# Loading the first two batches' queries and keys in fp32 into unused accumulators, and writing out the order of the attention and first-expert steps

## The chip, the core and the metric

One core of a Trainium2 chip. The metric is the device time of one execution in microseconds (us); lower is better.

## The reference, cut to what matters

Attention with exponential features of both signs, then a mixture of eight experts whose weights P come from eight rounds of row and column normalisation.

```python
# q, k, v: (8 batches, 8 heads, 576, 64) fp32;  w_phi: (64, 128)
def phi(x):
    proj = einsum('bhsd,df->bhsf', x, w_phi)
    proj = proj - max(abs(proj), axis=-1)
    return concatenate([exp(proj), exp(-proj)], axis=-1)
q_p, k_p = phi(q), phi(k)
kv = einsum('bhsf,bhsd->bhfd', k_p, v);  z = sum(k_p, axis=2)
x = einsum(q_p, kv) / (q_p . z + 1e-6)          # reshaped to (4608, 512)
# P: softmax-like table (4608, 8), normalised 8 times over rows and columns
for e in range(8):
    out += P[:, e:e+1] * (maximum(x @ w1[e], 0) @ w2[e])   # 512 -> 1024 -> 512
```

## The kernel before

The kernel records every operation with an estimated duration and its dependencies in a plan. A list scheduler, run when the kernel is built, then writes the program: it repeatedly takes the operation that can start earliest by its model, and among equals the one recorded first. So each engine's instruction order is fixed at build time. It depends on the order of recording and on the modelled durations of everything, loads included. On the chip each engine runs its own list in order and waits where it must.

Work is cut into 32 pairs of heads (four per batch). The 576 rows are taken as 512 plus a rest of 64; the rests of a whole batch are handled together. For each pair: scores, maxima and exponentials of keys and queries (`pair_a`), GpSimd's products of v with the maxima's exponentials, the key-value sums and outputs (`pair_b`), and the transposed x (`pair_c`). Expert 0 runs between the pairs as fill: 24 "up" steps and 20 "down" steps.

```python
# loads: cast fp32 -> bf16 on the way, so issued from GpSimd, into 2 staging buffers
def load_qk(b, hh, nh, t, r=()):
    for x, src in ((1, k), (0, q)):
        dma("POOL", nh << 17, 230, lambda ...: nc.gpsimd.dma_start(
            out=t["qk"]()[:, x, o:o + nh], in_=src[b, hh:hh + nh, 0:SM]....))
ring(a_in, [128, 2, 4, NJ * D], BF16, "qk", 2)
...
# batches 0 and 1: transposed by TensorE in bf16; later batches by a DMA transpose
if b < 2:
    for x in (1, 0):
        ptr = new("P1")
        for c in range(4):
            pe(128, ... nc.tensor.transpose(bf(ptr)[:, c*128:(c+1)*128], t["qk"]()[...], ident) ...)
        dve(256, ... nc.vector.tensor_copy(out=t["T"]()[...], in_=bf(ptr)[:, 0:512]) ...)
...
# one fixed pattern of steps: a = pair_a (+ rest_a), e = one up and one down of expert 0
for i in range(NS + AD + 1):
    for s in "aebc":
        if s == "a" and i < NS: stage_a(i)
        elif s == "e" and i - LAG < 4 * NA + 4: expert0(i - LAG)     # LAG = 7
        elif s == "b": stage_b(i - AD)                                # AD = 1
        elif s == "c": stage_c(i - AD - 1)
```

The five accumulators `acc[0..4]` (128 x 4 x 512 fp32 each) lie unused until expert 0's first down step writes one.

## Time and profile before

| | before |
|---|---|
| time, median of 4 runs beside the changed kernel | 1053.74 us (1051.75 to 1054.75) |
| TensorE idle from 0 to 90 us | 21.5 us |
| GpSimd busy from 0 to 25 us | 21.7 us |
| second products of pair 0 / pair 8 / pair 31 start on GpSimd | 10.7 / 70.6 / 222.3 us |
| first matmul of expert 1's weights on x | 274.2 us |

All rows but the first come from one profiled execution of 1056.06 us.

The page of the kernel before, its span and first part (busy us and share of the span for TensorE = PE, its weight loads = PEld, VectorE = DVE, ScalarE = ACT, GpSimd = POOL):

```profile
span 1054.0 us, 24517 instructions
...
PE 1022.4 (97%) x9512; PEld 841.3 (80%) x9512; DVE 824.6 (78%) x1634; ACT 707.8 (67%) x1560; POOL 475.4 (45%) x551
...
```

The windows view of the kernel before. Columns are named in its first line; "PEclk" is the granted TensorE clock.

```profile
...
core 0: us, PE busy (x) PEld busy (x) DVE busy (x) ACT busy (x) POOL busy (x), PEclk, DMA share, GB/s
0.00:25.00 25.00, 14.51 (x136) 9.22 (x137) 14.80 (x35) 13.44 (x34) 21.69 (x42) 1.00 0.90 135
0.00:90.00 90.00, 68.45 (x734) 43.52 (x735) 72.69 (x179) 68.99 (x180) 66.48 (x128) 0.96 1.03 154
90.00:220.00 130.00, 128.71 (x1423) 83.68 (x1421) 116.37 (x284) 120.27 (x309) 79.38 (x159) 1.00 0.79 129
220.00:270.00 50.00, 48.55 (x308) 24.40 (x307) 42.29 (x114) 17.98 (x36) 3.25 (x6) 0.97 0.36 119
300.00:1054.00 754.00, 749.75 (x6834) 668.28 (x6831) 569.66 (x1021) 470.77 (x983) 320.45 (x254) 1.00 0.27 69
...
```

From 90 us on TensorE is nearly always busy. All that is loose lies in the first 90 us, where four engines are each at 74 to 81%. GpSimd is the one that is full at the very start: 21.7 of 25 us.

The chain of waits of the kernel before (start, length, what):

```profile
...
3.57 1.79 POOL qk_r L367 x3
5.36 6.26 DMA qk_r<-in_q_dram
...
19.66 0.61 POOL vrd_89 L440
...
46.76 0.97 POOL qk_r L367 x2
...
50.63 0.72 POOL qk_r L367
...
61.23 10.31 DMA qkT<-qk
...
```

TensorE's rests hang on a q load that GpSimd could only issue at 5.36 us, behind other loads, and that landed at 11.6 us. Then GpSimd's own products and load issues are on the chain at 20 us and at 46 to 51 us, and a DMA transpose at 61 to 71 us.

The clock's records in this trace show half clock until 15.4 us, again from 25.7 to 32.5 us and from 230.5 to 233.9 us. The view's PEclk column cannot show the first of these, since the records begin with the change to full clock; the pitch of the matmuls does (0.43 us per 512 columns, 0.22 later).

### The profile page before, as it was taken

What the parts mean: (1) busy time and instruction counts of PE and PEld (TensorE: products, weight loads), DVE (VectorE), ACT (ScalarE), POOL (GpSimd) and SP (SyncE); (2) the same over time, 40 slices, a digit from 0 to 9 for tenths busy, and PEclk for the clock granted to TensorE, in tenths of its full rate; (3) what the DMA queues carried; (4) which work ended last, traced back from release to release, by engine and by line L of the source; (5) the groups of instructions that cost most, each with busy time, mean ns of one, the idle gap of its engine ahead of it and who ended that gap; (6) DMA issues with size and microseconds to landing.
All of it is one profiled execution on the core that took longest, in us unless ns stands there. A gap on an engine that the chain in (4) does not pass through costs nothing.

```text
span 1054.0 us, 24517 instructions
## 1 busy us (share of the span) xinstructions
PE 1022.4 (97%) x9512; PEld 841.3 (80%) x9512; DVE 824.6 (78%) x1634; ACT 707.8 (67%) x1560; POOL 475.4 (45%) x551
## 2 busy tenths in 40 slices
PE   5889999999899999999999999999999999999998
PEld 3546666654588888888888888888888888888886
DVE  6889988988867787778877787778777877777775
ACT  5789989954896656666666666665666666666663
POOL 8776755510044344334444444444333544434442
PEclk9899999999999999999999999999999999999999
DMA  9998886914511133113411341116111521114333
GB/s 143 141 187 133 136 142 121 159 47 164 101 41 47 48 89 81 41 51 81 89 43 41 76 86 42 49 46 127 41 41 51 111 61 42 41 41 128 114 131 120
DMA packets 105236, 91.57 MB, mean 87 GB/s; under 512 B 45344, under 2 KB 80288, under 8 KB 105120
## 3 DMA queue, kind: packets, MB, share of 16 engines
q1 hardware_dynamic: 65040, 63.78, 22.3%
q0 software_dynamic: 40080, 26.23, 18.2%
q8 instruction: 74, 1.21, 0.5%
q14 instruction: 42, 0.34, 0.1%
HBM read 94.98 MB, written 14.16 MB: 104 GB/s over the span
## 4 chain that ended last, share of the span: by engine, by line
PE 89%; ACT 4%; DVE 3%; DMA 2%; POOL 1%; issue 1%; DVEq 0%; ACTq 0%; POOLq 0%
DVE m L376 1%; DMA qkT<-qk 1%; ACT U L1027 1%; DMA qk_r<-in_q_dram 1%; DVE xb L590 0%; PE P_13550 L999 0%; PE P_12438 L999 0%; PE P_8591 L999 0%; PE P_15513 L999 0%; PE P_14556 L999 0%; PE P_14095 L999 0%; PE P_13743 L999 0%; PE P_13392 L999 0%; PE P_13188 L999 0%; PE P_12788 L999 0%
## 5 line engine op out<-in xcount | busy, mean ns | idle before, releaser
L999 PEld LDWEIGHTS <-S 128*128 128x128 bf16 x1984 | 194.1, 98 | 22.9 <-issue 0.5
L999 PEld LDWEIGHTS <-T 128*128 128x128 bf16 x1512 | 147.9, 98 | 20.4 <-issue 3.2
L999 PEld LDWEIGHTS <-hT 128*128 128x128 bf16 x1488 | 145.6, 98 | 16.9
L907 DVE TENSOR_TENSOR S<-hT 128x1024 bf16<-128x1024 bf16 x124 | 80.3, 684 | 0.0
L1155 POOL TENSOR_TENSOR acc_77<-acc_77,V 128x512 f32<-128x512 f32 x28 | 36.3, 1308 | 54.6 <-ACT V L1152 54.5
L1155 POOL TENSOR_TENSOR acc_78<-acc_78,V 128x512 f32<-128x512 f32 x28 | 37.4, 1349 | 49.0 <-ACT V L1152 48.9
L1155 POOL TENSOR_TENSOR acc_81<-acc_81,V 128x512 f32<-128x512 f32 x28 | 35.6, 1276 | 51.0 <-ACT V L1152 50.5
L1155 POOL TENSOR_TENSOR acc_4738<-acc_4738,V 128x512 f32<-128x512 f32 x28 | 35.5, 1274 | 51.1 <-ACT V L1152 50.5
L1155 POOL TENSOR_TENSOR acc_4740<-acc_4740,V 128x512 f32<-128x512 f32 x28 | 35.2, 1268 | 51.3 <-ACT V L1152 51.2
L1155 POOL TENSOR_TENSOR acc_80<-acc_80,V 128x512 f32<-128x512 f32 x28 | 35.4, 1269 | 49.9 <-ACT V L1152 49.3
L1155 POOL TENSOR_TENSOR acc_4737<-acc_4737,V 128x512 f32<-128x512 f32 x28 | 35.6, 1277 | 49.0 <-ACT V L1152 48.4
L1155 POOL TENSOR_TENSOR acc_79<-acc_79,V 128x512 f32<-128x512 f32 x28 | 35.8, 1289 | 48.1 <-ACT V L1152 47.6
L384 PEld LDWEIGHTS <-hT 128*128 128x128 bf16 x320 | 30.7, 101 | 26.6 <-issue 2.2
L1155 POOL TENSOR_TENSOR acc_4739<-acc_4739,V 128x512 f32<-128x512 f32 x24 | 30.4, 1273 | 37.3 <-ACT V L1152 36.9
L384 PEld LDWEIGHTS <-w_449 128*128 128x128 bf16 x288 | 26.1, 98 | 24.0 <-issue 2.9
L907 DVE TENSOR_TENSOR S<-S,hT 128x1024 bf16<-128x1024 bf16 x62 | 42.5, 685 | 0.8
L907 DVE TENSOR_TENSOR S<-hT,S 128x1024 bf16<-128x1024 bf16 x62 | 42.3, 682 | 0.0
L384 PEld LDWEIGHTS <-qkT 128*128 128x128 bf16 x256 | 24.4, 102 | 20.6 <-DVE xb_r L595 4.4
L999 PEld LDWEIGHTS <-w_3831 128*128 128x128 bf16 x288 | 28.2, 98 | 4.2 <-issue 0.7
L999 PEld LDWEIGHTS <-w_13099 128*128 128x128 bf16 x288 | 28.2, 98 | 3.3
L999 PEld LDWEIGHTS <-w_11515 128*128 128x128 bf16 x288 | 28.2, 98 | 3.3
L999 PEld LDWEIGHTS <-w_5153 128*128 128x128 bf16 x288 | 28.2, 98 | 3.3
(4017 smaller groups left out, 3296.2 us busy)
## 6 DMA issues: line engine op xcount, KB each, us to landing
v_m<-in_v_dram SPq DMA_DIRECT2D x15, 512.0 KB, 5.4
qk<-in_k_dram POOLq DMA_DIRECT2D x15, 256.0 KB, 5.1
qk<-in_q_dram POOLq DMA_DIRECT2D x15, 256.0 KB, 5.8
X<-xd_98 SPq DMA_DIRECT2D x7, 256.0 KB, 2.6
X<-xd_99 SPq DMA_DIRECT2D x7, 256.0 KB, 2.7
X<-xd_100 SPq DMA_DIRECT2D x7, 256.0 KB, 2.7
X<-xd_101 SPq DMA_DIRECT2D x7, 256.0 KB, 3.1
X<-xd_102 SPq DMA_DIRECT2D x7, 256.0 KB, 2.6
```

The lines of the kernel that those rows point to most:

```text
L376: dve(el, lambda: nc.vector.tensor_reduce(out=dst(), in_=src(), axis=AX.X, op=ALU.max, apply_absolute_value=True), r, w)
L384: nc.tensor.matmul(out_, lhsT=lhsT, rhs=rhs, start=start, stop=stop)
L907: lambda: f.tensor_tensor(out=out_(), in0=x(), in1=y(), op=op), r, w, **kw)
L999: pe(256, lambda i=i, k=k, z=z: nc.tensor.matmul(bank()[:, 256 * i:256 * i + 256], lhsT=lhs(k, i), rhs=rhs(k), start=first and z, stop=k = ...
L1027: act(512, lambda: nc.scalar.copy(out=u[fp][n]().rearrange("p a b -> p (a b)"), in_=x[fp]()), [x[fp]], [u[fp][n]])
L1155: pool(670, lambda: nc.gpsimd.tensor_tensor(out=acc[g][:, 2 * i:2 * i + 2, 256 * j:256 * j + 256], in0=acc[g][:, 2 * i:2 * i + 2, 256 * j: ...
```

## The change

Intent: take q and k of batches 0 and 1 off GpSimd and its two staging buffers. They land as fp32 in accumulators that are not needed yet, by plain loads from SP, and TensorE transposes fp32 data; the copy out of PSUM rounds to bf16. ScalarE takes the copies of q. Besides that, `pair_a` is split into a key part and a query part, and the fixed pattern gives way to a written string of steps (a keys, q queries, r rests, b, c, g gate, u up, d down).

```diff
+        if b < 2:
+            g = t["f"]                       # 4 - 2*b - i: acc[4], acc[3], acc[2], acc[1]
+            for x, src in ((1, k), (0, q)):
+                i = 2 * x + o // 2
+                dma("SP", nh << 17, 320, lambda x=x, src=src, i=i: nc.sync.dma_start(
+                    out=acc[g][:, i:i + nh // 2]...., in_=src[b, hh:hh + nh, 0:SM]....),
+                    r, [("acc", g, 2 * x + n) for n in keys])
+            return
@@ the rests of batches 0 and 1: the same, into acc[0]
@@ pair_a
-                    pe(128, ... nc.tensor.transpose(bf(ptr)[...], t["qk"]()[...], ident) ...)
-                dve(256, ... nc.vector.tensor_copy(out=t["T"]()[...], in_=bf(ptr)[:, 0:512]) ...)
+                    pe(128, ... nc.tensor.transpose(
+                        ptr()[:, c*128:(c+1)*128], acc[g][:, i, c*128:c*128+128], identf) ...)
+                if x:
+                    dve(512, ... nc.vector.tensor_copy(out=t["T"]()[...], in_=ptr()) ...)
+                else:
+                    act(512, ... nc.scalar.copy(out=t["T"]()[...], in_=ptr()) ...)
@@ start
-    dma("SP", ... nc.sync.dma_start(out=wphi_f[...], in_=w_phi))        # twice
+    dma("ACT", ... nc.scalar.dma_start(out=wphi_f[...], in_=w_phi))     # twice
-    dma("POOL", ... nc.gpsimd.dma_start(out=wgate, in_=moe_w_gate...))
+    dma("SP", ... nc.sync.dma_start(out=wgate_f, in_=moe_w_gate...))
+    act(32, lambda: nc.scalar.copy(out=wgate, in_=wgate_f), ["wgate_f"], ["wgate"])
@@ order
-    for i in range(NS + AD + 1):
-        for s in "aebc": ...
+    order = (
+        "aqraqabbcqabqacbqrbcaqbacuqaqbacqruabgqccucbudbduaqabdqadgrcbucqucabqcauqdua"
+        "bgcbqaducdcqubcrbaudqauqdacbcdqduardqbbgcubuaqcaubgcdqacdqabubruqadbqadcbqbu"
+        "cagcquaubqrdbadqaudbcqcaucbdcccqbgcg"
+    )
+    for i, n in enumerate(order):
+        STEPS[n](order[:i].count(n))
```

Left out: branches of the form `if 2 == 0` that are removed and never ran, an identity in fp32 of which ScalarE makes the bf16 copy, and a swap at the start: the q and k loads of the second pair of heads are now recorded before those of the rests.

More of the change, by code (lines that the diff above doesn't have):

```diff
@@ L216 @@
     ident = a_in.tile([128, 128], BF16, name="ident")
+    identf = a_in.tile([128, 128], FP32, name="identf")
+    wgate_f = a_in.tile([128, NP, E], FP32, name="wgate_f")
     wphi_f = a_in.tile([128, DF], FP32, name="wphi_f")
@@ L322, in load_qk @@
         keys = [o // 2] if nh == 2 else [0, 1]
+        if b < 2:
[3 more added lines that the diff above has]
+                dma("SP", nh << 17, 320, lambda x=x, src=src, i=i: nc.sync.dma_start(
+                    out=acc[g][:, i:i + nh // 2].rearrange("p a (h c) -> p (a h) c", h=2),
+                    in_=src[b, hh:hh + nh, 0:SM].rearrange("h (p j) d -> p h (j d)", j=NJ)),
+                    r, [("acc", g, 2 * x + n) for n in keys])
+            return
         for x, src in ((1, k), (0, q)):
@@ L351, in turn_qk, with new_half @@
                     [(t["qk"], x, i)], [(t["T"], x, i)])
-    def new_half():
-        return {"qk": new("qk"), "T": new("qkT"), "v": new("v_m")}
+    def new_half(b, i):
+        t = {"T": new("qkT"), "v": new("v_m")}
+        if b < 2:
+            return {"f": 4 - 2 * b - i, **t}
+        return {"qk": new("qk"), **t}
     def load_rests(b0, nb, r=()):
-        t = {"qk": new("qk_r"), "v": new("v_r"), "b0": b0}
+        t = {"v": new("v_r"), "b0": b0}
+        if b0 >= 2:
+            t["qk"] = new("qk_r")
         for h in range(2):
@@ L365, in load_rests @@
             for x, src in ((1, k), (0, q)):
+                if b0 < 2:
+                    dma("SP", 1 << 16, 150, lambda rows=rows, x=x, src=src, part=part:
+                        nc.sync.dma_start(out=acc[0][rows, b0].rearrange(
+                            "p (a x d) -> p a x d", a=NP, x=2)[:, :, x], in_=part(src)),
+                        r, [("acc", 0, b0, h, x)])
+                    continue
                 dma("POOL", nb << 16, 90, lambda rows=rows, x=x, src=src, part=part:
@@ L390, in rest_a @@
         rT = new("rT")
-        rk = [(t["qk"], h, x) for h in range(2) for x in range(2)]
+        if b >= 2:
+            rk = [(t["qk"], h, x) for h in range(2) for x in range(2)]
         if b < 2:
@@ L395, in rest_a @@
                 pe(128, lambda pr=pr: nc.tensor.transpose(
-                    bf(ptr)[:, pr * 128:pr * 128 + 128],
-                    t["qk"]()[:, bi + pr].rearrange("p a b -> p (a b)"), ident),
-                    rk + ["ident"], [ptr])
-            dve(256, lambda: nc.vector.tensor_copy(
-                out=rT().rearrange("p a b -> p (a b)"), in_=bf(ptr)[:, 0:512]), [ptr], [rT])
+                    ptr()[:, pr * 128:pr * 128 + 128],
+                    acc[0][:, b, pr * 128:pr * 128 + 128], identf),
+                    [("acc", 0, b, h, x) for h in range(2) for x in range(2)] + ["identf"],
+                    [ptr, ("acc", 0, b)])
+            dve(512, lambda: nc.vector.tensor_copy(
+                out=rT().rearrange("p a b -> p (a b)"), in_=ptr()), [ptr], [rT])
         else:
@@ L453, in pair_a @@
         if b < 2:
+            g = t["f"]
             for x in (1, 0):
                 ptr = new("P1")
+                i = 2 * x + h0 // 2
                 for c in range(4):
-                    pe(128, lambda x=x, c=c, ptr=ptr: nc.tensor.transpose(
-                        bf(ptr)[:, c * 128:(c + 1) * 128],
-                        t["qk"]()[:, x, h0 + c // 2, (c % 2) * 128:(c % 2) * 128 + 128],
-                        ident), [(t["qk"], x, h0 // 2), "ident"], [ptr])
-                dve(256, lambda x=x, ptr=ptr: nc.vector.tensor_copy(
-                    out=t["T"]()[:, x, 2 * h0:2 * h0 + 4, :].rearrange("p a b -> p (a b)"),
-                    in_=bf(ptr)[:, 0:512]), [ptr], [(t["T"], x, h0 // 2)])
+                    pe(128, lambda c=c, i=i, ptr=ptr: nc.tensor.transpose(
+                        ptr()[:, c * 128:(c + 1) * 128], acc[g][:, i, c * 128:c * 128 + 128],
+                        identf), [("acc", g, i), "identf"], [ptr])
+                if x:
+                    dve(512, lambda x=x, ptr=ptr: nc.vector.tensor_copy(
+                        out=t["T"]()[:, x, 2 * h0:2 * h0 + 4, :].rearrange("p a b -> p (a b)"),
+                        in_=ptr()), [ptr], [(t["T"], x, h0 // 2)])
+                else:
+                    act(512, lambda x=x, ptr=ptr: nc.scalar.copy(
+                        out=t["T"]()[:, x, 2 * h0:2 * h0 + 4, :].rearrange("p a b -> p (a b)"),
+                        in_=ptr()), [ptr], [(t["T"], x, h0 // 2)])
         def qkT(x, c, n):
@@ L507, in pair_a, with queries @@
                 out=s["v"][y]()[:, :, D], in_=em()), [em], [(s["v"][y], 1)])
-        mq = scores(0, 1)
-        for p0 in range(0, 2, 1):
-            pt = new("P1")
-            for par in range(1):
-                pe(512, lambda par=par, p0=p0, pt=pt: mm(
-                    pt()[:, 512 * par:512 * par + 512], wphi2[:, p0 + par, :], qkT(0, 0, 4),
-                    True, True), [(t["T"], 0, h0 // 2), "wphi2"], [pt])
-            for y, sg in ((0, 1.0), (1, -1.0)):
-                exp(512 * 1, lambda y=y, p0=p0: s["T"][y]()[:, p0:p0 + 1].rearrange(
-                    "p a b c -> p (a b c)"), lambda pt=pt: pt(), sg, [pt], [(s["T"][y], p0)])
-        exp(10, lambda: s["r"]().rearrange("p (a b) -> p a b", a=2)[:, :, 0:4],
-            lambda: m()[:, 0].rearrange("p (a b) -> p a b", a=2), -2.0,
-            mq, [(s["r"], 0)])
         s["Ek"] = [[(s["E"][y], c0) for c0 in range(0, 4, 2 * 1)] for y in range(2)]
         s["Tk"] = [[(s["T"][y], p0) for p0 in range(0, 2, 1)] for y in range(2)]
-        return s
+        def queries():
+            mq = scores(0, 1)
+            for p0 in range(0, 2, 1):
+                pt = new("P1")
+                for par in range(1):
+                    pe(512, lambda par=par, p0=p0, pt=pt: mm(
+                        pt()[:, 512 * par:512 * par + 512], wphi2[:, p0 + par, :], qkT(0, 0, 4),
+                        True, True), [(t["T"], 0, h0 // 2), "wphi2"], [pt])
+                for y, sg in ((0, 1.0), (1, -1.0)):
+                    exp(512 * 1, lambda y=y, p0=p0: s["T"][y]()[:, p0:p0 + 1].rearrange(
+                        "p a b c -> p (a b c)"), lambda pt=pt: pt(), sg, [pt], [(s["T"][y], p0)])
+            exp(10, lambda: s["r"]().rearrange("p (a b) -> p a b", a=2)[:, :, 0:4],
+                lambda: m()[:, 0].rearrange("p (a b) -> p a b", a=2), -2.0,
+                mq, [(s["r"], 0)])
+        return s, queries
     def pair_b(b, pr, s, r):
@@ L690, in down0 @@
     def down0(g, part):
-        if 1 == 2 and part % 2:
-            return
-        tss = (part, part + 1) if 1 == 2 else (part,)
+        tss = (part,)
         py = down(W[0][1], hts[g], tss, akey(g))
@@ L714 @@
         for i in range(2):
-            halves[b, i] = new_half()
+            halves[b, i] = new_half(b, i)
     load_qk(0, 0, 2, halves[0, 0])
-    dma("SP", 1 << 15, 100, lambda: nc.sync.dma_start(out=wphi_f[0:64, :], in_=w_phi),
+    dma("ACT", 1 << 15, 100, lambda: nc.scalar.dma_start(out=wphi_f[0:64, :], in_=w_phi),
         w=["wphi_f0"])
-    dma("SP", 1 << 15, 100, lambda: nc.sync.dma_start(out=wphi_f[64:128, :], in_=w_phi),
+    dma("ACT", 1 << 15, 100, lambda: nc.scalar.dma_start(out=wphi_f[64:128, :], in_=w_phi),
         w=["wphi_f1"])
     load_v(0, 0, 2, halves[0, 0])
-    if 2 == 0:
-        turn_qk(halves[0, 0], 0)
-    pool(300, lambda: make_identity(nc, ident), w=["ident"])
+    pool(300, lambda: make_identity(nc, identf), w=["identf"])
+    act(128, lambda: nc.scalar.copy(out=ident, in_=identf), ["identf"], ["ident"])
     dve(128, lambda: nc.vector.memset(wphi2, 0.0), w=["wphi2"])
@@ L729 @@
             [f"wphi_f{i}"], ["wphi2"])
+    load_qk(0, 2, 2, halves[0, 0])
     load_rests(0, 1)
-    load_qk(0, 2, 2, halves[0, 0])
     load_v(0, 2, 2, halves[0, 0])
-    if 2 == 0:
-        turn_qk(halves[0, 0], 1)
     load_qk(0, 4, 4, halves[0, 1])
     load_v(0, 4, 4, halves[0, 1])
-    if 2 == 0:
-        turn_qk(halves[0, 1])
     for i in range(2):
@@ L743 @@
     dve(128, lambda: nc.vector.memset(colw, float(E) / float(N)), w=["colw"])
-    dma("POOL", 1 << 14, 50, lambda: nc.gpsimd.dma_start(
-        out=wgate, in_=moe_w_gate.rearrange("(c p) e -> p c e", p=128)), w=["wgate"])
-    LAG = 7
-    rs, st = {}, {}
+    dma("SP", 1 << 14, 50, lambda: nc.sync.dma_start(
+        out=wgate_f, in_=moe_w_gate.rearrange("(c p) e -> p c e", p=128)), w=["wgate_f"])
+    act(32, lambda: nc.scalar.copy(out=wgate, in_=wgate_f), ["wgate_f"], ["wgate"])
+    rs, st, qs = {}, {}, {}
     W[0] = (new("w1"), new("w2"))
-    def expert0(i):
-        if i < 0 or i >= (4 * (0 or NG) + 4):
-            return
-        plan.prio = 0
-        if i < (4 * (0 or NG)):
-            up0(i // 4, i % 4)
-        if i >= 4:
-            down0(i // 4 - 1, i % 4)
-        plan.prio = 0
     def stage_a(i):
         b, pr = i // 4, i % 4
-        st[i] = pair_a(b, pr, halves[b, pr // 2])
-        if pr == 0:
-            rs[b] = rest_a(b, rests[b])
+        st[i], qs[i] = pair_a(b, pr, halves[b, pr // 2])
         gt = [("max", 0, i - 1)] if i >= 1 else []
@@ L768, in stage_a @@
             if b + 1 > 1:
-                halves[b + 1, pr // 2] = new_half()
+                halves[b + 1, pr // 2] = new_half(b + 1, pr // 2)
             t = halves[b + 1, pr // 2]
@@ L777, in stage_a, with stage_r, stage_g, expert0 @@
         n = i - 2
-        if 0 <= n < 8 * 1 and n % 1 == 0:
-            for y in range(1):
-                if 1 * (n // 1) + y < 8:
-                    load_w0(1 * (n // 1) + y, [("max", 0, i - 1)] if i >= 1 else [])
-    NS = 4 * B
+        if 0 <= n < 8:
+            load_w0(n, gt)
     xbs = {}
-    AD = 1
+    def stage_r(b):
+        rs[b] = rest_a(b, rests[b])
     def stage_b(j):
-        if 0 <= j < NS:
-            xbs[j] = pair_b(j // 4, j % 4, st[j], rs[j // 4])
-    def stage_c(j):
-        if 0 <= j < NS:
-            pair_c(j // 4, j % 4, xbs[j])
-            if j % 4 == 3:
-                rest_c(j // 4, rs[j // 4])
-                gate(j // 4)
-    for i in range(NS + AD + 1):
-        for s in "aebc":
-            if s == "a" and i < NS:
-                stage_a(i)
-            elif s == "e" and i - LAG < 4 * NA + 4:
-                expert0(i - LAG)
-            elif s == "b":
-                stage_b(i - AD)
-            elif s == "c":
-                stage_c(i - AD - 1)
-    gate(8)
-    fill = range(min(NS + AD + 1 - LAG, 4 * NA + 4), 40)
+        xbs[j] = pair_b(j // 4, j % 4, st[j], rs[j // 4])
+    def stage_g(b):
+        rest_c(b, rs[b])
+        gate(b)
+    STEPS = {"a": stage_a, "q": lambda i: qs[i](), "r": stage_r, "b": stage_b,
+             "c": lambda j: pair_c(j // 4, j % 4, xbs[j]), "g": stage_g,
+             "u": lambda i: up0(i // 4, i % 4), "d": lambda i: down0(i // 4, i % 4)}
+    order = (
[5 more added lines that the diff above has]
+        STEPS[n](order[:i].count(n))
+    gate(8)
+    def expert0(i):
+        if i < 4 * NG:
+            up0(i // 4, i % 4)
+        down0(i // 4 - 1, i % 4)
+    fill = range(4 * NA + 4, 4 * NG + 4)
     def swap():
@@ L944, in sums_w @@
         t1, t1k = q(w2, *b12), k(w2, *b12)
-        if 1 and e == E - 1:
+        if e == E - 1:
             T[0] = new("T")
@@ L977, in sums_x @@
                            (3, b21, x(1), [1])):
-            sub(dve if g in (0,1,2,3,4,5,6,7,8) else pool, 512, x(n), y, z, ALU.subtract,
+            sub(dve, 512, x(n), y, z, ALU.subtract,
                 xkeys(g) + ["late"] + [(X[i // 2], i % 2) for i in r]
@@ L1205 @@
     dn = None
-    for e in range(0 if 0 else 1, E):
-        w1, w2 = load_w(e, [("xT", 5, 3)]) if e else W[0]
-        if e == (0 if 0 else 1):
-            for g in (0,1,2,3,4,5,6,7,8):
+    for e in range(1, E):
+        w1, w2 = load_w(e, [("xT", 5, 3)])
+        if e == 1:
+            for g in range(NG):
                 sums_x(g)
         A7, B7 = sums_w(e, w1, w2)
-        for g in (range(0, NG) if e == 0 else range(NG) if e < E - 1 else [8, *range(8)]):
+        for g in (range(NG) if e < E - 1 else [8, *range(8)]):
             X = load_x(g)
@@ L1222 @@
                 dn["out"]()
-            if 1 and e == E - 1 and g == 7:
+            if e == E - 1 and g == 7:
                 down8(e, g, hT, w2)
@@ L1226 @@
                 dn = down7(e, g, hT, B7)
-    if not 1:
-        for n in ORDER:
-            if len(n) == 2:
-                dn[n]()
-        dn["out"]()
     plan.run(tc)
```

## The prediction

> **What bounds the kernel.** Engine totals: TensorE busy 1022 of 1054 us. The windows view splits this: from 300 us on 749.8 of 754 us at granted clock 1.00 (experts 1 to 7), from 90 to 220 us 128.7 of 130. These stages are TensorE-bound; the change leaves their work alone. Only 0 to 90 us is loose: 21.5 us of TensorE idle, and part of its busy time at half speed (512-column matmuls 0.43 us apart up to 15 us and near 25 to 32 us, 0.22 later; granted clock 0.57 in 25 to 30 us). At the warm rate the work there is some 51 us (my estimate). VectorE is busy 72.7 us of the 90, ScalarE 69.0, GpSimd 66.5: nothing is full, waits pass between engines. Pairs 0 to 7 take about 8.3 us each (pair 8's queries reach TensorE at 71.6 us), later pairs about 6.2, though they carry expert work too.
>
> **What holds that stage.** The chain of waits: the rests' q load (issued 5.4 us, landed 11.6, behind GpSimd's serial queue), then ScalarE, GpSimd's products (to 22.8 us), GpSimd issues and products at 46 to 52 us, and 10.3 us of a DMA transpose before 71.5 us. GpSimd is 87% busy in 0 to 25 us; each cast load costs it 0.63 to 0.85 us of issue. Second-batch q/k loads, waiting for two staging buffers, go out only at 15 to 37 us.
>
> **What the change does.**
> - 16 q/k loads and wgate leave GpSimd: 17 x 0.72 = 12 us of its time in the first 50. The Trainium skill (DMA: Bandwidth & Descriptors, SWDGE vs HWDGE vs iDMA) says a casting DMA must come from GpSimd; the trace agrees, only plain loads are on SP. Fp32 needs no cast, so SP can issue. Idle accumulators also remove the staging wait.
> - TensorE gains 18 groups of four fp32 transposes. None is in the trace; the fp32 column-sum matmul there runs as two passes with 0.19 us weight loads against 0.10 for bf16. I estimate 0.3 to 0.8 us more per group, 5 to 14 us in all, nearly wholly inside the idle 0 to 65 us.
> - VectorE: K copies grow from 0.42 to about 0.69 us (like its 512-column fp32 PSUM reads), 8 q copies leave: about -1 us. ScalarE gains 8 x 0.60 = 5 us.
> - Written order: same work (24 up, 20 down steps). Queries become separate steps, batch 0 runs ahead of the rests, expert steps come in bursts. After 90 us little idle is left to win (1.3 us to 220, 1.5 in 220 to 270).
>
> **Sum.** Early pairs should drop from 8.3 to about 7 us: 8 to 12 us saved, half-speed clock included; 2 us more from ordering later; 1 to 3 us returned by the fp32 transposes. Net 11 us, 1.0%.
>
> Predicted 1043 us, 80% range 1033.5 to 1051. Faster by over 2%: 0.1; within 2%: 0.88; slower: 0.02.
>
> **What would show it.** TensorE idle in 0 to 90 us falls from 21.5 to about 12 us; GpSimd busy in 0 to 25 us below 15 us; pair 8's queries on TensorE near 62 us; no 6 us wait on the rests; batch-1 loads issued before 20 us; the expert stage unchanged, its start (265 to 270 us) about 11 us earlier.
>
> **What would make it wrong.** Fp32 transposes dearer than 1.5 us per group, at half clock; VectorE already the real limit of the early pairs (88% in 25 to 80 us), so gain under 5 us; SP's serial issue (0.6 us each) delaying v or the rests; or the order working so well that 20 us go.

## More of the kernel before

The timeline of GpSimd in the kernel before, the two k loads of batch 1 (their q loads follow directly, at 15.79 and 24.29 us):

```profile
...
15.04 0.76 POOL L324 DMA_DIRECT2D qk<-in_k_dram  x1 [1.89 <-PE P_240 L457]
...
23.54 0.76 POOL L324 DMA_DIRECT2D qk<-in_k_dram  x1
...
```

Each costs GpSimd 0.76 us of issue, and they go out at 15.0 and 23.5 us.

## The result

| | before | after |
|---|---|---|
| median (4 runs each) | 1053.74 us | 1044.93 us (1044.55 to 1046.51) |
| ratio, 95% interval | | 0.9922 (0.9907 to 0.9937) |
| ratio in a later repeat on another chip | | 0.9909 (0.9895 to 0.9922) |
| TensorE idle, 0 to 90 us | 21.5 us | 14.4 us |
| GpSimd busy, 0 to 25 us | 21.7 us | 9.6 us |
| second products of pair 0 / 8 / 31 | 10.7 / 70.6 / 222.3 us | 11.4 / 65.5 / 211.5 us |
| first matmul of expert 1's weights on x | 274.2 us | 263.2 us |

A ratio is the mean time of one kernel's runs over the mean of the other's runs of the same rounds, so it is not quite the ratio of the medians in the table.

The page of the changed kernel:

```profile
span 1043.5 us, 24529 instructions
...
PE 1020.4 (98%) x9512; PEld 842.1 (81%) x9512; DVE 823.9 (79%) x1626; ACT 711.1 (68%) x1570; POOL 461.5 (44%) x532
...
```

The windows view of the changed kernel, columns as above:

```profile
...
0.00:25.00 25.00, 16.37 (x142) 12.23 (x142) 16.09 (x34) 17.26 (x43) 9.59 (x25) 1.00 0.93 248
0.00:90.00 90.00, 75.63 (x819) 50.69 (x820) 77.75 (x184) 78.46 (x204) 59.55 (x121) 1.00 1.02 189
90.00:220.00 130.00, 128.49 (x1455) 83.16 (x1452) 117.21 (x296) 119.01 (x306) 75.46 (x152) 1.00 0.76 123
220.00:270.00 50.00, 49.03 (x262) 25.47 (x261) 43.31 (x106) 26.17 (x46) 1.70 (x2) 1.00 0.54 146
300.00:1043.00 743.00, 739.01 (x6738) 658.93 (x6735) 565.11 (x1008) 458.16 (x958) 314.64 (x250) 1.00 0.27 70
...
```

TensorE is busy 7.2 us more in the first 90 us (3.0 us of that is the fp32 transposes, 11.2 us against 8.2 for the bf16 ones), VectorE and ScalarE have gained too, and GpSimd does less than half of what it did in the first 25 us. Expert 1 starts 11 us earlier in these two traces, and the rest of the span is alike.

The chain of waits of the changed kernel:

```profile
...
2.77 6.68 DMA acc<-in_q_dram
...
11.00 6.41 DMA wgate_f<-in_moe_w_gate_dram
...
17.43 0.22 ACT wgate L775
...
30.93 1.80 DVE m L399 x3
...
59.37 2.52 PE P L407 x30
...
```

Up to 68 us GpSimd is gone from this chain (its products for the rests stand there from 68.2 to 70.0 us, in lines left out here), and so is the 10 us DMA transpose; at 59 us, in the time of that transpose, TensorE's own matmuls stand. Two of the first lines are landings that SP or ScalarE waited for, and the wait for the gate weights is a new one (tested below).

The timeline of SP in the changed kernel, the first and the last of batch 1's loads:

```profile
...
11.58 1.02 SPq L329 DMA_DIRECT2D acc<-in_k_dram  x1
...
20.75 0.37 SPq L329 DMA_DIRECT2D acc<-in_q_dram  x1
...
```

They go out at 11.6 to 20.8 us, where the kernel before sent them at 15 to 24 us, and none waits for GpSimd.

The transposes and the copy out of PSUM, in the timeline of the kernel before:

```profile
...
12.80 0.42 DVE L461 COPY qkT<-P_222 128x512 bf16<-128x512 bf16 x1
...
16.59 0.39 PE L457 MATMUL P_294<-ident,qk 128*128 128x128 bf16 x4
...
```

and in that of the changed kernel:

```profile
...
9.80 0.68 DVE L488 CAST qkT<-P 128x512 bf16<-128x512 f32 x1
...
20.87 1.07 PE L484 MATMUL P<-identf,acc 128*128 128x128 f32 x8 [0.24 <-ACT r L403]
...
```

At full clock four bf16 transposes start 0.055 us apart; eight fp32 ones fill 1.07 us with a pitch of 0.109 us. The copy of 512 columns grew from 0.42 to 0.68 us. The Trainium skill (VectorE: DVE Perf Modes, Why PSUM operands drop a tier) says that fp32 read from PSUM runs without the packed mode that bf16 may use; these two durations agree with it.

### The profile page after: what moved, and what is told of

Same layout as the page of the kernel before. It is cut to its first block, busy times and chain, and to the rows that moved or that the text cites. A ratio compares the mean times of both kernels' runs of the same rounds, so it can differ in the third digit from the quotient of the medians.

```text
span 1043.5 us, 24529 instructions
## 1 busy us (share of the span) xinstructions
PE 1020.4 (98%) x9512; PEld 842.1 (81%) x9512; DVE 823.9 (79%) x1626; ACT 711.1 (68%) x1570; POOL 461.5 (44%) x532
## 4 chain that ended last, share of the span: by engine, by line
PE 89%; ACT 5%; DVE 3%; DMA 1%; issue 1%; SPq 0%; POOL 0%; DVEq 0%; ACTq 0%
PE P L1019 70%; PE P L407 16%; ACT acc L1181 2%; DVE m L399 1%; PE P L606 1%; ACT k L403 1%; DMA acc<-in_q_dram 1%; DMA wgate_f<-in_moe_w_gate_dram 1%; ACT V L1171 1%; ACT U L1047 1%; PE P L645 1%; DVE xb L626 0%; ACT q L403 0%; DVE P L618 0%; PE P L484 0%
## 5 line engine op out<-in xcount | busy, mean ns | idle before, releaser
L1174 POOL TENSOR_TENSOR acc<-acc,V 128x512 f32<-128x512 f32 x248 | 316.4, 1283 | 440.4 <-ACT V L1171 437.2
L1051 DVE CUSTOM_DVE_ANT_0 hT<-P,U 128x512 bf16<-128x512 f32 x378 | 255.0, 687 | 107.9 <-ACT U L1047 59.7
L1047 ACT COPY U<-P 128x512 f32<-128x512 f32 x378 | 217.8, 590 | 137.4 <-PE P L1019 130.8
L1171 ACT ACTIVATE V<-P,P 128x256 f32<-128x256 f32 x496 | 206.3, 477 | 123.4 <-PE P L1019 121.6
L1159 DVE SCALAR_TENSOR_TENSOR acc<-P,P,acc 128x256 f32<-128x256 f32 x372 | 160.1, 478 | 73.4 <-PE P L1019 71.7
L1019 PEld LDWEIGHTS <-w 128*128 128x128 bf16 x2016 | 197.3, 98 | 23.7 <-issue 0.6
L1019 PE MATMUL P<-X,w 128*128 128x256 bf16 x1008 | 154.7, 273 | 0.4 <-ACT U L1047 0.4
L1019 PE MATMUL P<-xT,w 128*128 128x256 bf16 x1008 | 152.0, 273 | 0.0
L1019 PE MATMUL P<-X,T 128*128 128x256 bf16 x1008 | 148.6, 273 | 1.3 <-ACT U L1047 1.2
L1019 PE MATMUL P<-w,hT 128*128 128x256 bf16 x992 | 142.6, 273 | 0.6 <-DVE hT L1051 0.6
L532 POOL TENSOR_TENSOR v<-v_m,em 128x512 bf16<-128x512 f32 x64 | 66.8, 1043 | 70.6 <-ACT em L403 57.5
## 6 DMA issues: line engine op xcount, KB each, us to landing
w<-in_moe_w_dram POOLq DMA_DIRECT2D x14, 1024.0 KB, 10.4
```

The lines of the kernel that those rows point to most:

```text
L532: pool(512, lambda y=y, em=em: nc.gpsimd.tensor_tensor(out=s["v"][y]()[:, :, 0:D], in0=t["v"]()[:, h0:h0 + 2].rearrange("p a (b c) -> p (a ...
L1019: pe(256, lambda i=i, k=k, z=z: nc.tensor.matmul(bank()[:, 256 * i:256 * i + 256], lhsT=lhs(k, i), rhs=rhs(k), start=first and z, stop=k = ...
L1047: act(512, lambda: nc.scalar.copy(out=u[fp][n]().rearrange("p a b -> p (a b)"), in_=x[fp]()), [x[fp]], [u[fp][n]])
L1051: dve(500, lambda: nc.vector._custom_dve(ADD_SAT, out=out_(fp, i, j), in0=bank[fp]().rearrange("p (a b) -> p a b", a=2), in1=u[fp][n](), s ...
L1159: dve(330, lambda n=n, ts=ts: nc.vector.scalar_tensor_tensor(out=acc[g][:, ts, 256 * j:256 * j + 256], in0=bank()[:, 256 * n:256 * n + 256 ...
L1171: act(390, lambda n=n: nc.scalar.activation(out=u()[:, n, :], in_=bank()[:, 256 * n:256 * n + 256], func=ACT.Copy, bias=0.0, scale=P[:, 4 ...
```

## The experiments

Times are medians; ratios are against the kernel before, run in the same rounds. The changed kernel stands at 0.9922 and 0.9909. In the names, "same order" means that every engine's instructions stand as in the changed kernel. The only differences are those stated.

| run | time | ratio, 95% interval |
|---|---|---|
| e1: loads only | 1053.58 | 0.9996 (0.9979 to 1.0012) |
| e2: order only | 1055.00 | 1.0004 (0.9992 to 1.0015) |
| h1: loads, written order for the first third | 1047.93 | 0.9934 (0.9920 to 0.9947) |
| e3: GpSimd issues, rescheduled | 1051.04 | 0.9963 (0.9950 to 0.9976) |
| f3: GpSimd issues, same order | 1049.55 | 0.9953 (0.9939 to 0.9966) |
| e4: two landing places, rescheduled | 1059.75 | 1.0050 (1.0038 to 1.0062) |
| f2: two landing places, same order | 1044.88 | 0.9904 (0.9891 to 0.9918) |
| f1: transposes twice, same order | 1048.57 | 0.9938 (0.9925 to 0.9951) |
| c0: changed kernel again | 1044.63 | 0.9909 (0.9895 to 0.9922) |
| i1: two early waits taken away | 1045.67 | 0.9919 (0.9906 to 0.9933) |
| w1: before, with dummy matmuls first | 1054.72 | 1.0005 (0.9991 to 1.0019) |
| w2: i1, with dummy matmuls first | 1046.16 | 0.9924 (0.9912 to 0.9936) |

The first theory was that the loads open the first 80 us and the written order adds as much again later, each on its own. The rivals were that one of the two does it all.

### e1: the loads alone

The changed kernel with the old sequence of steps.

```diff
-    order = ("aqraqabbc...")
+    order = ""
+    for i in range(34):
+        order += "aq" * (i < 32) + "r" * (i < 32 and i % 4 == 0)
+        order += "u" * (7 <= i < 31) + "d" * (11 <= i < 31)
+        order += "b" * (1 <= i < 33) + "c" * (i >= 2) + "g" * (i >= 2 and i % 4 == 1)
```

> The changed loads, landing places, fp32 transposes and copies, with the step order of the kernel before. Theory (the loads open the first 80 us, the written order gives about as much again later): about 5 us below the kernel before, near 1049 us (ratio 0.993 to 0.997), with pairs 0 to 8 as early as in the changed kernel and pair spacing after that as before. Rival 1 (loads give everything, order nothing): 1044 to 1046 us. Rival 2 (the order gives everything): 1053 to 1055 us.

Measured: 0.9996, no gain outside the noise; the interval allows 2 us at most. The timed runs spread from 1051.75 to 1058.53 us, the slowest at the lowest mean clock (0.993), so the profiled run (span 1051.1 us) is one of the better ones. The windows view of it:

```profile
...
0.00:25.00 25.00, 16.86 (x150) 12.67 (x151) 16.85 (x36) 18.04 (x45) 10.44 (x27) 1.00 0.94 257
0.00:90.00 90.00, 71.23 (x761) 47.00 (x762) 75.09 (x178) 75.84 (x198) 56.74 (x114) 1.00 1.04 188
215.00:235.00 20.00, 18.55 (x184) 10.83 (x183) 16.95 (x47) 7.59 (x19) 2.44 (x5) 0.91 0.19 68
...
```

GpSimd is as free at the start as in the changed kernel (10.4 of 25 us), and TensorE is as busy there. Still, only 2.8 us of the 7.2 us of extra TensorE time up to 90 us are there, less than the 3.1 us that the fp32 transposes add in this trace. Nor are the early pairs as early as in the changed kernel: the second products of pair 8 start at 67.2 us against 65.5, and those of pair 31 at 219.5 against 211.5. Near 225 us there is the half-clock stretch of the kernel before. Its chain of waits at 36 to 41 us:

```profile
...
36.72 0.72 POOL w L311
...
37.46 0.63 POOL vrd L465
...
38.29 0.61 POOL vrd L465
...
39.94 0.61 POOL vrd L465
...
40.98 0.58 DVE P L618
...
```

GpSimd's issue of a weight load and the four products of batch 1's rests stand in front of VectorE's next step, one after another, with the loads long landed. The old sequence walks into GpSimd's queue elsewhere. Both theory (5 us) and the rival that the loads do it all fall.

### e2: the written order alone

The kernel before with the query part split off and the written string, cast loads and bf16 transposes kept.

> The written order with the cast loads, bf16 transposes and copies of the kernel before. Theory: about 4 to 6 us below before, near 1049 us, if the two parts add. Rival (the order was written around the new loads and starves on the old ones): at or above 1053 us. If this and the loads-only run sum to much less or more than 8.2 us the parts depend on each other.

Measured: 1.0004. The rival named there is borne out: nothing is gained on the old loads. The windows view of this run:

```profile
...
0.00:25.00 25.00, 14.26 (x131) 9.01 (x132) 13.99 (x32) 13.96 (x36) 21.83 (x42) 1.00 0.90 137
...
```

GpSimd is as full as before, and TensorE no busier. The two parts sum to nothing, and together they give 9 us: the gain is in their interaction. One thing was not tried: an order written for the old loads. So the runs do not say what a good order alone could give, only that this one gives nothing there.

### h1: which part of the order

Changed loads; the written string up to the key step of the 13th pair, then the remaining steps in the old sequence.

```diff
-    for i, n in enumerate(order):
-        STEPS[n](order[:i].count(n))
+    first, then = numbered(order), numbered(old)       # old: as in e1
+    first = first[:first.index(("a", 12))]
+    for n, i in first + [x for x in then if x not in first]:
+        STEPS[n](i)
```

> The changed loads, the written order up to the 13th pair's first step, the remaining steps in the sequence of before. Theory (the written order pays chiefly between 35 and 100 us, where the lost TensorE time falls by 7 us against loads alone, and a further 3 us at 215 to 235 us where it avoids a gap and a half-clock stretch): 1047 to 1049 us, TensorE time lost before 100 us as in the changed kernel, the gap near 225 us back. Rival (the order only pays at the end of attention): 1052 us or more.

Measured: 0.9934, about 7 us below the kernel before, where e1 is at 0.4 us. So the first third of the order is worth about 6.5 us given the new loads; the rest of it, from h1 to the changed kernel, about 3 us. The windows view of h1:

```profile
...
0.00:90.00 90.00, 75.50 (x802) 50.48 (x811) 78.23 (x185) 79.35 (x207) 59.88 (x122) 1.00 1.05 190
215.00:235.00 20.00, 18.31 (x158) 9.92 (x158) 17.35 (x51) 5.40 (x12) 1.56 (x5) 1.00 0.37 129
...
```

and the last stretch in the changed kernel:

```profile
...
215.00:235.00 20.00, 20.00 (x143) 10.36 (x139) 17.86 (x51) 7.29 (x14) 0.00 (x0) 1.00 0.44 158
...
```

TensorE's first 90 us are those of the changed kernel (75.5 against 75.6 us), and the gap at the end of attention is back: 1.7 us idle at 215 to 235 us against none. Both halves of the expectation hold, except that the clock did not fall there this time.

### e3 and f3: who issues the loads

e3 gives the fp32 loads back to GpSimd in the plan (`"SP"` to `"POOL"`, `nc.sync` to `nc.gpsimd`), so the scheduler also writes a different order. f3 changes only the issuing engine of the emitted instruction (`nc.sync` to `nc.gpsimd`) and keeps the rest of the program.

> The changed kernel, but its fp32 q and k loads of batches 0 and 1 are issued from GpSimd again (no cast, same accumulators, same order). Theory (what the loads give is GpSimd's issue time and serial queue): loses most of the loads' gain, 3 to 6 us slower than the changed kernel, 1048 to 1051 us. Rival (the gain comes from the free landing places and larger packets, not from who issues): within 1.5 us of the changed kernel.

> The changed kernel with every other instruction in its order, the fp32 q and k loads issued from GpSimd at the same places of the program. Theory (GpSimd's issue time, 16 x 0.7 us ahead of its products, is what the loads remove): 4 to 8 us slower than the changed kernel, first products about 4 us later, a half-clock stretch near 25 to 35 us again. Rival (the 6 us seen with GpSimd issuing came from a different order too): within 2 us of the changed kernel.

Measured: e3 1051.04 us, f3 1049.55 us. Against f2, which ran beside f3 and equals the changed kernel (below), f3 is 4.7 us slower. The windows view of f3:

```profile
...
0.00:25.00 25.00, 12.55 (x89) 9.26 (x90) 13.69 (x26) 14.68 (x38) 19.52 (x38) 1.00 0.85 226
...
```

GpSimd is back to 19.5 of 25 us, and pair 0's second products start at 14.6 instead of 11.4 us; pair 8's at 69.1 instead of 65.5. So about half of the gain hangs on which engine issues these loads. It is not shown that this is GpSimd's issue time ahead of its products. The first line below is of f3's timeline of TensorE, the second of its timeline of GpSimd:

```profile
...
5.84 1.09 PE L484 MATMUL P<-identf,acc 128*128 128x128 f32 x4 [5.84 <-DMA acc<-in_k_dram]
...
```

```profile
...
12.71 1.04 POOL L532 TENSOR_TENSOR v<-v_m,em 128x512 bf16<-128x512 f32 x1 [3.74 <-ACT em L403]
...
```

Before its first product GpSimd was not issuing: it had been idle for 3.7 us, waiting for ScalarE, because q and k came late. TensorE's first transposes waited for k until 5.84 us, in f2 until 3.66 us, and the last load of batch 0's rests landed at 14.1 us, in f2 at 10.3. It had left only 0.6 us later (6.67 against 6.06 us). What else changed is the queue of SP: without the q and k loads it sent v ahead (the 512 KB v load of batch 0 left at 3.55 us, in f2 at 10.12; in the kernel before at 4.66). Only at 20.7 and 22.3 us do GpSimd's load issues stand between its products in f3's chain of waits. So the 4.7 us hold the later landing of q and k and GpSimd's time together, and no run separates them. The expected half-clock stretch near 25 to 35 us did not return in f3 (it did in e3, at 28.5 to 35.3 us), so it is not needed for the loss.

### e4 and f2: where the loads land

e4 lets batch 1 land in batch 0's two accumulators.

```diff
-            return {"f": 4 - 2 * b - i, **t}
+            return {"f": 4 - i, **t}
```

f2 does the same to the addresses alone (`acc[g + 2 * (g < 3)]` in the load and in the transpose), leaving the plan, and so the order, as it was.

> The changed kernel, but batch 1 lands in the same two accumulators as batch 0, so its loads wait until batch 0 has been transposed, as with the two staging buffers of the kernel before. Theory (the issue time matters, the waiting does not, since batch 0 is transposed by about 21 us): within 1.5 us of the changed kernel. Rival (idle accumulators are what matters): 3 us or more slower.

> As the run in which batch 1 lands in batch 0's two accumulators, but with the order of every engine as in the changed kernel (only the addresses change). Theory (that run's 15 us came from the build-time scheduler, which modelled later landings and wrote another order, not from the waits): within 1.5 us of the changed kernel. Rival (the landing place itself costs): about 10 to 15 us slower, as there.

Measured: e4 is 1059.75 us, slower than the kernel before; f2 is 1044.88 us, the changed kernel. The windows views of e4 and of f2:

```profile
...
40.00:60.00 20.00, 13.90 (x127) 9.65 (x126) 13.48 (x31) 12.57 (x34) 13.28 (x25) 0.76 0.77 95
...
```

```profile
...
40.00:60.00 20.00, 17.65 (x209) 11.65 (x211) 18.57 (x50) 17.79 (x45) 18.01 (x33) 1.00 1.44 178
...
```

The addresses and the waits that come with them are the same in both. What differs is the order: told of a later landing, the scheduler wrote a program in which TensorE idles 6 us in these 20 us and the clock drops to 0.76. e4's expectation fell for its theory, and its rival seemed right, but f2 shows why neither was: e4 measured the scheduler. The idle accumulators are thus not needed for their freedom. Batch 0 is turned in time, and two landing places would do, provided that the program stays as written.

### f1: are the fp32 transposes on the path?

Each of the pairs' 64 fp32 transposes is emitted twice inside one planned operation, so that the order stays.

> The changed kernel with the order of every engine kept as it is, and each of the 64 fp32 transposes of the pairs done twice. The added TensorE work is 64 x 0.109 us = 7.0 us at full clock. Theory (early TensorE is not full, so most of it hides): 1 to 3 us slower than the changed kernel. Rival (once the loads are early the fp32 transposes are on the path and eat part of the gain): 5 to 8 us slower, which would also mean that the 3.8 us that fp32 costs over bf16 are paid.

Measured: 1048.57 us, 3.7 us above f2 of the same rounds, for 7.0 us of added TensorE work. About half is paid, a little above the theory's 1 to 3 us and below the rival's 5 to 8. Scaled to the change (72 transposes, each 0.109 instead of 0.055 us at full clock, 3.9 us in all), fp32 turning costs some 2 us of the gain; this is an estimate from f1, since no version without that cost was run.

### i1, w1, w2: can more be had?

i1, in the same order otherwise: w_phi's first half goes out on SP ahead of everything (one queue each for the two halves), and ScalarE's cast of the gate weights moves to just before the first gate. w1: nine dummy matmuls of 512 columns on a tile of ones at the very start of the kernel before. w2: i1 with the same nine.

> The changed kernel itself, as the yardstick on this chip for the three runs beside it: 1044 to 1046 us, ratio 0.990 to 0.9925.

> Two waits that the changed kernel's own trace shows are taken away, all else in its order: ScalarE's cast of the gate weights waited 1.36 us at 17.4 us for a small DMA (it moves to just before the first gate), and the first TensorE scores waited 0.8 us at 6.5 us for the second half of w_phi (its two DMAs now go out at once on two queues). Theory: 1 to 2 us below the changed kernel. Rival (the first 20 us have slack that later waits swallow): within 0.7 us.

> The kernel before with 9 dummy 512-column matmuls at its very start, to end the half clock before 15.4 us. If half speed at the start is on the path: 2 to 4 us below before, full clock from 5 to 9 us. Rival (TensorE only waits for loads there, so its speed does not matter): within 1 us, though the clock comes earlier.

> The run with the two waits taken away, plus the 9 dummy matmuls. If the half clock up to 9.2 us costs the changed kernel anything: a further 1 to 1.5 us, in all 2 to 3 us below it, near 1042 us and the best version. Rival: no further gain.

Measured: c0 1044.63, i1 1045.67, w2 1046.16, w1 1054.72 us; no gain anywhere, and none of these is better than the changed kernel. Why i1 missed shows in the timelines of TensorE, of the changed kernel run again:

```profile
...
3.71 2.03 PE L484 MATMUL P<-identf,acc 128*128 128x128 f32 x8 [3.71 <-DMA acc<-in_k_dram]
5.83 1.47 PE L407 MATMUL P<-wphi,qkT 128*128 128x256 bf16 x8
...
```

and of i1:

```profile
...
4.82 1.94 PE L490 MATMUL P<-identf,acc 128*128 128x128 f32 x8 [4.82 <-DMA acc<-in_k_dram]
6.94 1.44 PE L413 MATMUL P<-wphi,qkT 128*128 128x256 bf16 x6 [0.18 <-DVE wphi L766]
```

The w_phi load took SP's first slot, so the first k load left 0.64 us later and TensorE started 1.1 us later. In the repeat of the changed kernel the wait for w_phi that i1 was to remove is not even there: the scores start at 5.83 us, where the first trace had 6.53. That wait was chance in one trace. The gate cast did move; whatever it freed did not reach the end.

In w1 the clock was full from 5.8 to 12.6 us, fell for 3.4 us, and was full again from 16.1 us, where the kernel before has half clock up to 15.4 us. The time did not change (0.9 us faster to 2.0 us slower), as the rival has it: in the kernel before, the speed of TensorE in the first 15 us is hardly what is waited for. The test is not quite clean, since the dummies themselves held the first transposes from 4.57 to 5.28 us and could hide a gain of that size. The same holds for w2: its first transposes started at 5.27 us, in i1 at 4.82, and its w_phi cast came behind their copy, at 7.1 us instead of 6.7.

What the half-clock stretches at 25 to 32 us and at 230 us cost the kernel before can be bounded from the run lists. The changed kernel's four traces of the same order (after, c0, f2, f1) have none between 9.3 us and the end. Of the nine executions of the kernel before beside c0, three have a mean granted clock of 1.000; a single stretch of 3.4 us at half clock would leave 0.998. (The start, before the first record, is not in this mean.) These three took 1053.34 to 1053.65 us, against a median of 1054.16 for all nine and 1044.63 for c0. So some 0.6 us of the 9.5 us between c0 and the kernel before go with the stretches, and about 9 us are there without them. This compares executions and is not an experiment: the runs of e1 order by clock too (1058.5 us at 0.993, 1051.8 us at 0.999), but a low clock also follows idle time (in e4 TensorE was busy for 0.75 of the 3.4 us before its clock fell at 50.4 us).

## Why the prediction was right, and where it was not

The time was: 1043 us predicted, 1044.9 measured, inside the range; "within 2%" was given 0.88. Point by point:

- **Where the slack is: right.** Only the first 90 us were loose. TensorE's idle time there fell from 21.5 to 14.4 us (predicted about 12), and expert 1 began 11.0 us earlier (predicted about 11). That this start agrees is luck in part: the profiled execution of the kernel before was a slow one, and against w1's trace the start is 8.7 us earlier, in line with the 8.8 us between the medians.
- **GpSimd's issue time: right that issuing there costs, the way only in part.** Its busy time in 0 to 25 us fell to 9.6 us (predicted below 15), and giving the issues back costs 4.7 us (f3). But much of that comes through q and k landing later, not through products held up behind issues. The loads that moved are 18, not 16. And the "15 to 37 us" of the second batch's loads took in the third batch's: batch 1's went out at 15.0 to 24.3 us, those of its rests from 11.9 us on.
- **Idle accumulators "also remove the staging wait": wrong as a cause.** f2 brings that wait back and loses nothing.
- **The sum: the step that failed.** The prediction added "8 to 12 us" for the loads' effect on the early pairs and "2 us more from ordering later". Measured, the loads alone give 0.4 us (interval 2 us faster to 1 us slower), the order alone nothing, both 9 us. Of these, 6.5 us come from the first third of the order (h1 against e1), which the prediction did not price at all, and about 3 us from the later part. The terms are not additive.
- **The early pairs' pace was misread.** "Pair 8's queries reach TensorE at 71.6 us" took pair 10's matmul for pair 8's: the query matmuls counted in order put pair 8 at 58.6 us before and 54.4 after, pair 10 at 71.6. Queries also run ahead of keys. By GpSimd's second products, pairs 0 to 8 took 7.5 us each before and 6.8 after ((70.6 - 10.7) / 8 and (65.5 - 11.4) / 8). The predicted fall of 1.3 us a pair was 0.7. The remaining gain came after pair 8: 5.1 us there, 10.8 at pair 31 (against w1's trace 3.3 and 8.8 us).
- **The fp32 transposes: estimated too dear, cost about right.** At full clock a group of four adds 0.22 us, not 0.3 to 0.8, so 3.9 us in all, not 5 to 14. They are not "nearly wholly" hidden: about half is paid (f1), some 2 us, within the 1 to 3 us that the sum allowed.
- **Copies: right.** 0.42 to 0.68 us on VectorE against 0.69 predicted, 0.58 to 0.64 us on ScalarE against 0.60.
- **Loads before 20 us: nearly.** The last of batch 1's q loads left at 20.75 us. The 6 us from the issue of the rests' last load to its landing are gone from the chain of waits; TensorE waited 0.57 us for the rests, before 2.43 us. Other landings of 6 us stand on the chain in their place.

So the size came out right partly because two errors offset each other: the loads by themselves were given far too much, and the order far too little.

## What to carry to other kernels

When a scheduler at build time turns one order and one set of modelled durations into a program, a change of a load changes the program too, and an order that was written for one set of loads may be worth nothing on another; test the two parts apart, and test a single cause with the instruction order frozen, or the scheduler is what gets measured (15 us between e4 and f2). Moving plain loads off an engine that also computes was worth half of 9 us here in the order written for it, and nothing in the old order; see in the trace whether the engine was really held up or its data only landed later, because moving the loads also changes which transfers go first. Check where the profiled execution lies among the timed ones before subtracting two traces (2 us here). Before removing a wait that one trace shows, see whether a second trace of the same program shows it.

## What the Trainium skill lacked or had wrong

- TensorE: Matmul & The Clock Gate, Part 4: PE-mode transpose, gives durations for bf16 alone. An fp32 128 x 128 transpose had a pitch of 0.109 us at full clock here, against 0.055 for bf16: eight of them took 1.07 us.
- The same page, What's actually happening, calls the clock's window free-running, so that the change to full clock varies by 0.5 us to either side. Three traces with the same TensorE program to that point (after, c0, f2) turned to full clock at 9.2, 6.8 and 8.2 us: a wider spread, about 2.5 us, though TensorE's first matmuls start within 0.1 us of each other; its later waits for loads vary between them. The table there has half clock come back after an idle window of about 3.4 us. Here no such window was idle: in the 3.4 us before the clock fell, TensorE was busy for 1.1 us in w1 (fall at 12.6 us) and for 2.2 us in the kernel before (fall at 25.7 us), while the changed kernel kept full clock after 3.4 us with 1.7 us busy (to 19.5 us).
- DMA: Bandwidth & Descriptors, Issuing engine by pattern and SWDGE vs HWDGE vs iDMA, say who may issue what, and under Issuing engines are not separate DMA queues that spreading issues saves sequencer time that "is usually small relative to the DMA itself". Here a load cost GpSimd 0.62 to 0.85 us, small against the 3.3 to 7.3 us from issue to landing in the kernel before, as the page has it. Still, issuing 18 of them from there costs 4.7 us (f3): it also changes which transfers go first, and k and q landed up to 3.8 us later.
- No page has a number for what a change of program order alone does: e4 and f2 differ by 15 us with the same work and the same addresses.
